# The down product of seven token pairs: another form of the seven-product scheme, with shared sums

## The chip, the core and the metric

The kernel runs on one core of a Trainium2 chip. The metric is the device time of one execution in microseconds; three runs of the kernel before gave 276.22, 276.23 and 276.27, median 276.23. The core has TensorE (PE in the profile, with its weight loads as PEld), VectorE (DVE), ScalarE (ACT), GpSimd (POOL) and SyncE (SP), which issues most of the transfers. Each engine works through its own list of instructions in order; waits between engines go over semaphores.

## The reference

Two layers on 2048 tokens of width 640, in bf16: a linear attention with 32 heads of width 20, and a gated product without a nonlinearity.

```python
qkv = layernorm(x) @ wqkv
phi_q = [softmax(q @ w_phi), softmax(-q @ w_phi)]        # per head; phi_k likewise
kv, z = sum over tokens of phi_k * v, of phi_k
o = (phi_q @ kv) / (phi_q @ z + 1e-6)
h = x + o @ wo
g, u = layernorm(h) @ w_gate, layernorm(h) @ w_up         # 640 -> 1536
out = h + (g * u) @ w_down                                # 1536 -> 640
```

The last line, the down product, is what is changed.

## The kernel before

Tokens are worked on in 16 tiles of 128, and the second layer in four blocks of four tiles (512 tokens). The work is cut into named units, and the names below are those of the lists in `ORDER`: `k`, `v` and `q` with a tile's number are its key, value and query products with their softmax, `K` and `Q` the sums and scalings of the feature maps, `A` the key-value product and `Aout` its copy, `n` the numerator and denominator of a tile, `h` its output product with the residual and the layer norm's statistics, `f0.3.2` the gate and up products of block 0, slice 3 of the hidden width (tokens from tile 2 of the block on), `T` the weight sums, `S` the block sums, `D1.0` the down product of the first pair of tiles in block 1, `d0` and `d1` the plain down product of tiles 0 and 1.

`ORDER` holds one list per engine, written out: the n-th occurrence of a unit's name on an engine is the n-th operation of that unit there. So it fixes the order on each engine in full. Nothing is moved at run time. Each operation carries a planned duration (`t`, `lat`) and `place` (L213) uses them to hand out buffers and to decide on which earlier operations each one waits; waits are made in `finish` (L302).

What the steps of the prediction touch:

- `fu` (L1068 on) makes one slice of the hidden layer: two products of five matmuls of 512 columns into one PSUM buffer of two banks, a copy of the gate half on ACT (L1077), the product of both on DVE (L1079). The buffer is free after DVE's step. There are four such buffers (`p_ps`), shared by all units.
- `queries` (L908 on): product, maximum and scaling on DVE (L872, L875), exponentials on ACT (L880), sums and reciprocal on DVE (L934, L940), two scalings on POOL (L941, L946).
- `num` (L992 on): products of 11 matmuls, then reciprocal (L1019) and scaling (L1021) on DVE.
- `watt` (L1027 on): output product of ten matmuls, two steps on DVE (L1050, L1053), square on ACT (L597), two steps on POOL (L1057, L1059, a power), the normalised rows `hb` on DVE (L1062), transposes issued by SP (L501).
- `weight_sums` (L1087): sums of quarters of `w_down` (768 x 320 each), one operation on POOL each (L1098), written into space that earlier weights and inputs leave.
- `block_sums` (L1101): sums of quarters of the hidden rows of a pair (each 128 tokens x 768), one operation on DVE each (L1110).
- `down_pair` (L1131): a pair's hidden rows (two tiles x two halves of the hidden width) times `w_down` (two halves x two halves of the columns) as a 2 x 2 block product by seven products instead of eight; a product is six matmuls of 320 columns (`mm`). Results that several blocks of the output need are copied from PSUM to `slot` by ACT (`snap`, L1161), combined on POOL (`padd`, L1167), and added to the remaining PSUM bank and written out by DVE (`fin`, L1172). A store of 160 KB per tile follows (L1177).

The pair of tiles 0 and 1 is done plainly (`down_raw`). In the form before, five block sums are made per pair, five weight sums in all, five copies per pair, and six additions on POOL per pair. Two of four last additions per pair wait for those on POOL.

Of the kernel before, what the change touches and what calls it, by code (L numbers as in the profile page):

```python
# [1318 lines left out]
```

## Time and profile before

| | |
|---|---|
| median of three runs | 276.23 us |
| profiled execution, first to last instruction | 274.27 us |
| TensorE busy | 266.2 us, 97% |
| VectorE busy | 202.0 us, 74% |
| ScalarE busy | 145.9 us, 53% |
| GpSimd busy | 147.9 us, 54% |
| granted TensorE clock | 1.000 |
| block sums (L1110) | 35, 23.7 us |
| copies (L1161) | 35, 15.3 us |
| weight sums (L1098) | 5, 19.3 us |

The profiled execution's own time is known by its span alone; the runs' times lie 1.96 us above it. A row of a group reads: line, engine, operation, written and read tiles, shapes, count, then busy time and the mean duration of one in ns, then the idle time ahead of it and what ended it. A row of the timeline reads: start and duration in us, engine, line, operation. The scratch tiles appear under the names of the memory that they lie in: the hidden rows as `phik`, block sums as `xT`, weight sums as `Wp` and `xT`, `w_down` as `vaug`, the copies as `eq` and `t`.

### The profile page before, as it was taken

What the parts mean: (1) busy time and instruction counts of PE and PEld (TensorE: products, weight loads), DVE (VectorE), ACT (ScalarE), POOL (GpSimd) and SP (SyncE); (2) the same over time, 40 slices, a digit from 0 to 9 for tenths busy, and PEclk for the clock granted to TensorE, in tenths of its full rate; (3) what the DMA queues carried; (4) which work ended last, traced back from release to release, by engine and by line L of the source; (5) the groups of instructions that cost most, each with busy time, mean ns of one, the idle gap of its engine ahead of it and who ended that gap; (6) DMA issues with size and microseconds to landing.
All of it is one profiled execution on the core that took longest, in us unless ns stands there. A gap on an engine that the chain in (4) does not pass through costs nothing.

```text
span 274.3 us, 5648 instructions
## 1 busy us (share of the span) xinstructions
PE 266.2 (97%) x2217; PEld 181.0 (66%) x2229; DVE 202.0 (74%) x388; ACT 145.9 (53%) x270; POOL 147.9 (54%) x187
## 2 busy tenths in 40 slices
PE   8999999999999999999999999999999999999992
PEld 8777776767868788788645557754554654456771
DVE  2899999999999989999855958555544565316772
ACT  3469999999676964776273422143342312332430
POOL 5437999999842365624899511621035330024895
PEclk9999999999999999999999999999999999999999
DMA  7988899803275897555564242620015101000112
GB/s 195 284 150 196 136 302 399 290 2 53 55 107 115 255 200 118 114 100 69 83 130 22 50 84 50 143 50 0 0 24 98 48 0 50 1 0 25 50 49 72
DMA packets 67099, 28.61 MB, mean 104 GB/s; under 512 B 57600, under 2 KB 65792, under 8 KB 67072
## 3 DMA queue, kind: packets, MB, share of 16 engines
q1 hardware_dynamic: 66144, 27.90, 44.9%
q10 hardware_dynamic: 928, 0.35, 0.5%
q8 instruction: 17, 0.28, 0.5%
q14 instruction: 10, 0.08, 0.1%
HBM read 11.82 MB, written 2.62 MB: 53 GB/s over the span
## 4 chain that ended last, share of the span: by engine, by line
PE 83%; POOL 6%; DVE 4%; DMA 2%; issue 2%; SPq 1%; ACT 1%; POOLq 0%; DVEq 0%
PE ps L604 83%; POOL eq L1167 4%; DMA Wp<-in_A_wqkv_dram 2%; POOL t L1167 2%; DVE ps L872 1%; DVE Sq L934 1%; SPq L501 1%; ACT phik L880 1%; DVE Ssum L894 0%; PE ps L512 0%; DVE Rk L896 0%; POOLq L371 0%; DVE x_all L1039 0%; DVE Phi L984 0%; SPq L497 0%
## 5 line engine op out<-in xcount | busy, mean ns | idle before, releaser
L604 PE MATMUL ps<-phik,Wgu 128*128 128x512 bf16 (+1 forms) x588 | 107.8, 335 | 0.6
L604 PEld LDWEIGHTS ps<-phik,Wgu 128*128 128x128 bf16 x600 | 58.1, 98 | 42.5 <-DVE phik L1079 1.2
L604 PE MATMUL ps<-Wp,xT 128*128 128x320 bf16 (+3 forms) x522 | 76.6, 299 | 0.2 <-ACT phik L880 0.2
L604 PEld LDWEIGHTS ps<-Wp,xT 128*128 128x128 bf16 x522 | 49.8, 98 | 19.5 <-ACT phik L880 0.7
L1079 DVE TENSOR_TENSOR phik<-ps,gate 128x512 bf16<-128x512 f32 (+1 forms) x60 | 34.0, 576 | 36.4 <-PE ps L604 29.9
L1077 ACT ACTIVATE gate<-ps 128x512 bf16<-128x512 f32 (+1 forms) x60 | 30.0, 511 | 53.8 <-PE ps L604 44.7
L897 POOL TENSOR_TENSOR phik<-phik,Rk 128x1280 bf16<-128x1280 bf16 x16 | 37.6, 2363 | 3.8 <-DVE Rk L896 3.0
L1167 POOL TENSOR_TENSOR eq<-eq 128x320 f32<-128x320 f32 x15 | 13.2, 881 | 33.1 <-ACT eq L1161 32.6
L872 DVE TENSOR_REDUCE ps<-ps 128x1 f32<-128x640 f32 (+1 forms) x32 | 26.1, 821 | 0.9 <-PE ps L604 0.3
L1161 ACT ACTIVATE eq<-ps 128x320 f32<-128x320 f32 x27 | 11.8, 438 | 27.0 <-PE ps L604 27.0
L1110 DVE TENSOR_TENSOR xT<-phik 128x768 bf16<-128x768 bf16 x35 | 23.7, 698 | 3.1 <-PE ps L604 3.1
L934 DVE TENSOR_REDUCE Sq<-eq 128x66 f32<-128x1320 bf16 x16 | 24.2, 1513 | 0.0
L894 DVE TENSOR_REDUCE Ssum<-phik 128x64 f32<-128x1280 bf16 x16 | 23.4, 1468 | 0.4 <-ACT phik L880 0.4
L1057 POOL TENSOR_SCALAR vpe<-shc 128x1 f32<-128x1 f32 x14 | 2.7, 192 | 36.4 <-ACT junk L597 36.1
L946 POOL TENSOR_TENSOR eq<-eq,rq 128x660 bf16<-128x660 bf16 x16 | 21.0, 1314 | 1.2
L597 ACT ACTIVATE junk<-x_all,nmh 128x640 bf16<-128x640 bf16 x14 | 11.6, 827 | 16.0 <-DVE x_all L1053 15.9
L880 ACT ACTIVATE eq<-ps,nb,rs 128x300 bf16<-128x300 f32 (+2 forms) x26 | 17.0, 687 | 5.4 <-DVE nb L875 4.6
L941 POOL TENSOR_TENSOR rq<-Sq,rq 128x33 f32<-128x33 f32 x16 | 4.5, 283 | 24.4 <-DVE rq L940 24.4
L604 PE MATMUL ps<-xT 128*128 128x320 bf16 (+1 forms) x144 | 17.4, 266 | 0.0
L880 ACT ACTIVATE eq<-ps,nb,nrs 128x300 bf16<-128x300 f32 (+2 forms) x26 | 17.2, 693 | 0.0
L880 ACT ACTIVATE phik<-ps,nb,rs 128x640 bf16<-128x640 f32 x16 | 14.2, 890 | 2.7 <-DVE nb L875 2.6
L604 PEld LDWEIGHTS ps<-xT 128*128 128x128 bf16 x144 | 11.8, 98 | 3.9 <-DVE xT L1110 0.2
(110 smaller groups left out, 374.9 us busy)
## 6 DMA issues: line engine op xcount, KB each, us to landing
x_all<-in_A_x_dram SPq DMA_DIRECT2D x4, 640.0 KB, 10.5
out_dram<-outb SPq DMA_DIRECT2D x16, 160.0 KB, 1.8
Wgu<-in_B_w_gate_dram SPq DMA_DIRECT2D x1, 1920.0 KB, 10.4
Wgu<-in_B_w_up_dram SPq DMA_DIRECT2D x1, 1920.0 KB, 15.8
vaug<-in_B_w_down_dram SPq DMA_DIRECT2D x1, 1920.0 KB, 9.0
Wp<-in_A_wqkv_dram SPq DMA_DIRECT2D x1, 800.0 KB, 4.9
phiqT<-in_A_wqkv_dram SPq DMA_DIRECT2D x1, 800.0 KB, 6.6
Wo<-in_A_wo_dram SPq DMA_DIRECT2D x1, 800.0 KB, 6.0
```

Of the source, the lines that this page charges most:

```text
L604: ins = e.matmul(o_, lhsT=l_, rhs=r_, start=s_, stop=p_, skip_group_check=True)
L872: g.op("DVE", lambda e: e.tensor_reduce(out=mx(), in_=src(), axis=AX.XY if len(src().shape) == 3 else AX.X, op=ALU.max, apply_absolute_val ...
L880: g.op("ACT", lambda e, s=s, sc=sc, to=to, of=of: e.activation(out=to(s), in_=of(), func=ACT.Exp, bias=nb[:, i:i + 1], scale=sc[:, t:t + 1 ...
L894: g.op("DVE", lambda e: e.tensor_reduce(out=Ssum[:, vs.i, :], in_=x, axis=AX.X, op=ALU.add), rd=R_phik[t], wr=vs.R, use=[vs], t=1.39, lat=1.5)
L897: g.op("POOL", lambda e: e.tensor_tensor(out=x, in0=x, in1=Rk[:, vr.i, :].unsqueeze(2).to_broadcast([P, 2 * H, DH]), op=ALU.mult), rd=vr.R ...
L934: g.op("DVE", lambda e: e.tensor_reduce(out=Sq[:, vs.i, :].rearrange("p (w g) -> p w g", w=NQ), in_=feat(0, NQ).rearrange("p w (g f) -> p ...
L946: return e.tensor_tensor(out=x, in0=x, in1=rq[:, vr.i, :].rearrange("p (w h) -> p w h", h=HW).unsqueeze(3).to_broadcast([P, NQ, HW, DH]), ...
L1077: g.op("ACT", lambda e: e.activation(out=gate[:, vg.i, 0:P * n], in_=PS[v.i][:, 0, 0:P * n], func=ACT.Copy), rd=[v.R[0]], wr=vg.R, use=[v, ...
L1079: g.op("DVE", lambda e: e.tensor_tensor(out=hhT[:, hb, ft, sl], in0=PS[v.i][:, 1, 0:P * n], in1=gate[:, vg.i, 0:P * n], op=ALU.mult), rd=[ ...
L1110: g.op("DVE", lambda e, k=k, x=x, y=y, op=op: e.tensor_tensor(out=SH[k][i], in0=part(x), in1=part(y), op=op), rd=rd, wr=[R_S[k][i]], t=0.6 ...
L1161: o = g.op("ACT", lambda e: e.activation(out=slot(x), in_=PS[v.i][:, bk, 0:HALF], func=ACT.Copy), rd=[v.R[bk]], wr=x.R, use=[v, x], after= ...
L1167: g.op("POOL", lambda e: e.tensor_tensor(out=slot(o_), in0=slot(a), in1=in1(), op=op), rd=a.R + r_, wr=o_.R, use=[o_, a] + ([y] if x is No ...
```

## The change

`down_pair` takes another form of the scheme, in which sums are built on each other: the third block sum uses the first, the fourth uses the third, and the weight sums likewise. There are four block sums per pair, four weight sums in all, seven products, and four copies per pair. The accumulation of products in one PSUM bank now makes most of the combinations: bank (v1, 0) takes products one, three and five one upon another and is copied after each. Each copy gets the residual added on POOL in place (one addition per copy, four per pair), and each of the four last additions on DVE reads one bank and one of those copies. The two stores of a pair change places. A copy may also be made by DVE, with the residual in the same step, where the table `SNAP` says so; it is empty, so all are made by ACT.

All five lists are new. On SP the loads keep their places; transposes and stores further on move with the units that they belong to. Three more edits: the weight and block sums take less of the old space (three weight slots and one in `xT`), the first exponential on ACT is counted as a user of the scratch tile it writes, and planned durations of the changed steps are set anew.

```diff
 def weight_sums():
-    for k, (a, b, op) in enumerate(((0, 3, ALU.add), (1, 3, ALU.subtract), (2, 0, ALU.subtract), (0, 1, ALU.add), (2, 3, ALU.add))):
+    for k, (a, b, op) in enumerate(((1, 0, ALU.subtract), (3, 1, ALU.subtract), (3, (0,), ALU.subtract), (2, (2,), ALU.subtract))):
...
 def block_sums(b, i):
-    for k, (x, y, op) in enumerate(((0, 3, ALU.add), (2, 3, ALU.add), (0, 1, ALU.add), (2, 0, ALU.subtract), (1, 3, ALU.subtract))):
+    for k, (x, y, op) in enumerate(((2, 3, ALU.add), (0, 2, ALU.subtract), ((0,), 0, ALU.subtract), (1, (2,), ALU.subtract))):
...
 def down_pair(b, i):
+    def snap(v, bk, t, half):
...
+        x.read = g.op("ACT", lambda e: e.activation(out=slot(x), in_=PS[v.i][:, bk, 0:HALF], func=ACT.Copy), rd=[v.R[bk]],
+                      use=[v, x], t=0.42, lat=0.55, **rw)
+        g.op("POOL", lambda e: e.tensor_tensor(out=slot(x), in0=slot(x), in1=x_all[:, t, c], op=ALU.add), rd=x.R + [R_h[t]],
+             wr=x.R, use=[x], t=0.87)
+        return x
+
+    def fin(v, bk, o_, half, y, after=None):
+        g.op("DVE", lambda e: e.tensor_tensor(out=outb[:, o_.i, HALF * half:HALF * (half + 1)], in0=PS[v.i][:, bk, 0:HALF], in1=slot(y),
+                                              op=ALU.add), rd=[v.R[bk]] + y.R, wr=[o_.R[half]], use=[v, o_, y],
+             after=[x.read for x in after or () if x.read], t=0.45, lat=0.57)
...
+    mm(v1, 0, raw(0), wraw(0), True, [v2])
+    a_ = snap(v1, 0, t1, 0)
+    mm(v2, 0, summed(0), wsum_(0), True)
+    d_ = snap(v2, 0, t2, 1)
+    mm(v1, 0, summed(2), wsum_(2), False)
+    b_ = snap(v1, 0, t1, 1)
+    mm(v1, 1, raw(1), wraw(2), True)
+    fin(v1, 1, o1_, 0, a_)
+    mm(v1, 0, summed(1), wsum_(1), False)
+    c_ = snap(v1, 0, t2, 0)
+    fin(v1, 0, o2_, 1, d_, [c_])
+    mm(v2, 1, raw(3), wsum_(3), True)
+    fin(v2, 1, o2_, 0, c_)
+    store(o2_, t2)
+    mm(v2, 0, summed(3), wraw(3), False)
+    fin(v2, 0, o1_, 1, b_)
+    store(o1_, t1)
```

The parts of the new lists that the prediction speaks of, from the place where block 1 begins to that of the first pair (`D0.1`):

```diff
 ORDER, "PE":
+ f1.10.0 f1.4.0 f1.10.0 f1.4.0 n14 f0.3.2 f0.3.2 h9 f1.3.0 f1.3.0 q13 f1.1.0 f1.1.0 f1.0.0 h14 f1.9.0 f1.0.0 f1.8.0 n11 f1.5.0
+ f1.9.0 f1.8.0 f1.7.0 f1.2.0 h10 f1.5.0 f1.2.0 n12 f1.7.0 d1 n13 f1.6.0 f1.6.0 h11 f1.11.0 f1.11.0 D0.1 D0.1 D0.1 n15 D0.1 D0.1 D0.1 D0.1
 ORDER, "DVE":
+ q15 f1.10.0 Q11 f0.0.2 Q15 n14 Q15 f0.3.2 S0.1.1 S0.1.0 h9 n14 f1.3.0 q13 h9 f1.4.0 q13 f1.1.0 h14 h14 S0.1.2 f1.0.0 n11 Q13 Q13 n11
+ f1.8.0 f1.9.0 S0.1.3 h9 h10 h10 f1.2.0 f1.7.0 n12 h8 f1.5.0 n13 d1 n12 n13 h10 h11 h11 f1.6.0 h11 n15 D0.1 f1.11.0
 ORDER, "ACT":
+ q15 q15 f1.10.0 q15 h8 f0.0.2 q15 d1 f0.3.2 f1.3.0 f1.4.0 f1.1.0 q13 h9 f1.0.0 q13 q13 q13 f1.8.0 f1.9.0 h10 f1.2.0 f1.5.0
 ORDER, "POOL":
+ Q12 Q12 Q11 h1 Q11 T0 h9 h9 T1 Q13 Q13 h8 Q15 Q15 h10 h10 h8 T2 T3 h11 h11 D0.1 D0.1 D0.1 h14 D0.1
```

In the lists before, POOL has `Q11 Q11 T2 T1 T0 h8 h8 T3 Q15` at this place and `T4` earlier, between `Q8` and `Q10`, and DVE has `S0.1.1 f0.5.0 S0.1.4` ahead of them and the next block sum, `S0.1.3`, after `f1.9.0`. At the end, the last two pairs are `D3.0` and `D3.1`; TensorE's new list ends with five products of the one and then the seven of the other; in the list before, the first two of `D3.1` stand among the last of `D3.0`.

More of the change, by code (lines that the diff above doesn't have):

```diff
@@ L58 @@
 ST_ACT = (12,)
+SNAP = {}
 SPLIT = [[(0, 2), (2, 2)], [(0, 4)], [(0, 4)], [(0, 4)]]
@@ L143, in __init__ @@
         self.R = [Reg() for _ in range(nreg)]
+        self.read = None
 class Op:
@@ L465, in _build @@
     Wkv = Wp[:, :, D:3 * D]
-    TW = [Wkv[:, 0:3, 0:2 * HALF], Wkv[:, 0:3, 2 * HALF:4 * HALF], Wkv[:, 3:5, 0:3 * HALF],
-          xTf[:, 0:KH * HALF].rearrange("p (a n) -> p a n", a=3), xTf[:, KH * HALF:2 * KH * HALF].rearrange("p (a n) -> p a n", a=3)]
-    o1 = 2 * KH * HALF
+    TW = [Wkv[:, 0:3, 0:2 * HALF], Wkv[:, 3:5, 0:3 * HALF], Wkv[:, 0:3, 2 * HALF:4 * HALF],
+          xTf[:, 0:KH * HALF].rearrange("p (a n) -> p a n", a=3)]
+    o1 = KH * HALF
     SH = [[xTf[:, o1 + KH * P * (2 * k + i):o1 + KH * P * (2 * k + i + 1)].rearrange("p (f n) -> p f n", f=KH) for i in range(2)]
-          for k in range(5)]
+          for k in range(4)]
     PS = [ctx.enter_context(nc.psum_tensor("ps%d" % i, [P, 2, 512], FP32)) for i in range(4)]
@@ L476, in _build @@
     p_hb, p_slot = Pool(2), Pool(8)
-    R_T, R_S = regs(5), [regs(2) for _ in range(5)]
+    R_T, R_S = regs(4), [regs(2) for _ in range(4)]
     SLOT_USERS = []
@@ L559, in _build @@
     pool_op(lambda e: e.memset(ones[:, :], SC / D), 0.2, wr=[R_one])
-    g.op("ACT", lambda e: e.activation(out=junk[:, 0, 0:1], in_=ones[:, 0:1], func=ACT.Exp), rd=[R_one], wr=[R_tab], t=1.4)
+    g.op("ACT", lambda e: e.activation(out=junk[:, 0, 0:1], in_=ones[:, 0:1], func=ACT.Exp), rd=[R_one], wr=[R_tab],
+         use=[Buf(p_junk)], t=1.4)
     pool_op(lambda e: e.memset(ident[:, :], 0.0), 0.2, wr=[R_id])
@@ L1087, in weight_sums, with part @@
         lo, hi = (0, HALF), (HALF, D)
-        for k, (a, b, op) in enumerate(((0, 3, ALU.add), (1, 3, ALU.subtract), (2, 0, ALU.subtract), (0, 1, ALU.add), (2, 3, ALU.add))):
-            U("T%d" % k)
-            def part(q, n):
-                f0, (c0, c1) = KH * (q // 2), (lo, hi)[q % 2]
-                return Wd[:, f0:f0 + KH, c0:c1].rearrange("p (a w) n -> p a w n", w=n)
-            def out_(n, k=k):
-                return TW[k].rearrange("p a (w n) -> p a w n", w=n)
+        def part(q, n):
+            if isinstance(q, tuple):
+                return TW[q[0]].rearrange("p a (w n) -> p a w n", w=n)
+            f0, (c0, c1) = KH * (q // 2), (lo, hi)[q % 2]
+            return Wd[:, f0:f0 + KH, c0:c1].rearrange("p (a w) n -> p a w n", w=n)
+        for k, (a, b, op) in enumerate(((1, 0, ALU.subtract), (3, 1, ALU.subtract), (3, (0,), ALU.subtract), (2, (2,), ALU.subtract))):
+            U("T%d" % k)
             n = TW[k].shape[2] // HALF
-            pool_op(lambda e, a=a, b=b, op=op, n=n, part=part, out_=out_: e.tensor_tensor(out=out_(n), in0=part(a, n), in1=part(b, n), op=op),
-                    4.0, rd=[R_Wd], wr=[R_T[k]])
+            rd = [R_Wd] + ([R_T[b[0]]] if isinstance(b, tuple) else [])
+            pool_op(lambda e, k=k, a=a, b=b, op=op, n=n: e.tensor_tensor(out=part((k,), n), in0=part(a, n), in1=part(b, n), op=op),
+                    4.0, rd=rd, wr=[R_T[k]])
     def block_sums(b, i):
@@ L1104, in part @@
         def part(q):
+            if isinstance(q, tuple):
+                return SH[q[0]][i]
             f0, c = KH * (q % 2), c0 + P * (q // 2)
             return hhT[:, hb_, f0:f0 + KH, c:c + P]
-        for k, (x, y, op) in enumerate(((0, 3, ALU.add), (2, 3, ALU.add), (0, 1, ALU.add), (2, 0, ALU.subtract), (1, 3, ALU.subtract))):
+        for k, (x, y, op) in enumerate(((2, 3, ALU.add), (0, 2, ALU.subtract), ((0,), 0, ALU.subtract), (1, (2,), ALU.subtract))):
             U("S%d.%d.%d" % (b, i, k))
-            rd = [R_hhT[hb_][ft][2 * i + q // 2] for q in (x, y) for ft in range(KH * (q % 2), KH * (q % 2) + KH)]
+            rd = [R_hhT[hb_][ft][2 * i + q // 2] for q in (x, y) if not isinstance(q, tuple)
+                  for ft in range(KH * (q % 2), KH * (q % 2) + KH)] + [R_S[q[0]][i] for q in (x, y) if isinstance(q, tuple)]
             g.op("DVE", lambda e, k=k, x=x, y=y, op=op: e.tensor_tensor(out=SH[k][i], in0=part(x), in1=part(y), op=op),
@@ L1157, in slot @@
             return eqf[:, HALF * x.i:HALF * (x.i + 1)] if x.i < 6 else t32[:, x.i - 6, :]
-        def snap(v, bk):
+        how = iter(SNAP.get((b, i), "AAAA"))
+        def snap(v, bk, t, half):
             x = Buf(p_slot)
-            o = g.op("ACT", lambda e: e.activation(out=slot(x), in_=PS[v.i][:, bk, 0:HALF], func=ACT.Copy), rd=[v.R[bk]], wr=x.R,
-                     use=[v, x], after=SLOT_USERS, t=0.42, lat=0.55)
-            return x, o
-        def padd(o_, a, y, op=ALU.add, x=None):
-            r_, in1 = (y.R, lambda: slot(y)) if x is None else ([R_h[x[0]]], lambda: x_all[:, x[0], HALF * x[1]:HALF * (x[1] + 1)])
-            g.op("POOL", lambda e: e.tensor_tensor(out=slot(o_), in0=slot(a), in1=in1(), op=op), rd=a.R + r_, wr=o_.R,
-                 use=[o_, a] + ([y] if x is None else []), t=0.72)
@@ L1170, in fin @@
-        def fin(v, bk, o_, t, y=None, after=()):
-            in1 = (lambda: slot(y)) if y is not None else (lambda: x_all[:, t, HALF * bk:HALF * (bk + 1)])
-            g.op("DVE", lambda e: e.tensor_tensor(out=outb[:, o_.i, HALF * bk:HALF * (bk + 1)], in0=PS[v.i][:, bk, 0:HALF], in1=in1(),
-                                                  op=ALU.add), rd=[v.R[bk], R_h[t]] + (y.R if y is not None else []), wr=[o_.R[bk]],
-                 use=[v, o_] + ([y] if y is not None else []), after=after, t=0.45, lat=0.57)
+            c = slice(HALF * half, HALF * (half + 1))
@@ new lines, in snap @@
+            rw = dict(wr=x.R, after=SLOT_USERS)
+            if next(how) == "V":
+                g.op("DVE", lambda e: e.tensor_tensor(out=slot(x), in0=PS[v.i][:, bk, 0:HALF], in1=x_all[:, t, c], op=ALU.add),
+                     rd=[v.R[bk], R_h[t]], use=[v, x], t=0.45, lat=0.57, **rw)
+                return x
+            x.read = g.op("ACT", lambda e: e.activation(out=slot(x), in_=PS[v.i][:, bk, 0:HALF], func=ACT.Copy), rd=[v.R[bk]],
+                          use=[v, x], t=0.42, lat=0.55, **rw)
@@ L1274, in _build @@
     each(queries, 3)
-    g.alias(R_T, R_Wp[1] + R_Wp[2] + R_xT[0:6])
+    g.alias(R_T, R_Wp[1] + R_Wp[2] + R_xT[0:3])
     weight_sums()
-    g.alias([r for x in R_S for r in x], R_xT[5:])
+    g.alias([r for x in R_S for r in x], R_xT[2:12])
     ffn(0)
```

24 lines of the change are left out of this document (1 added, 23 removed), and 96 rows, old and new, of the table ORDER.

## The prediction

> **What bounds the kernel now.** I read the page first, then the end of the timeline, then the timelines of VectorE (DVE) and GpSimd (POOL) beside each other, then the groups for durations.
>
> ```profile
> span 274.3 us, 5648 instructions
> PE 266.2 (97%) x2217; PEld 181.0 (66%) x2229; DVE 202.0 (74%) x388; ACT 145.9 (53%) x270; POOL 147.9 (54%) x187
> PE 83%; POOL 6%; DVE 4%; DMA 2%; issue 2%; SPq 1%; ACT 1%; POOLq 0%; DVEq 0%
> ```
>
> TensorE works 97% of the span and carries 83% of the chain, so whatever delays it adds to the time, and what other engines save is worth nothing by itself. The one stretch that it doesn't carry is the end, where the chain runs on POOL (6%). In timeline rows, the first number is the start, the second the duration:
>
> ```profile
> 265.60 0.98 PE L604 MATMUL ps<-Wp,phik 128*128 128x320 bf16 x6
> ...
> 266.41 0.98 PE L604 MATMUL ps<-vaug,xT 128*128 128x320 bf16 x6
> ...
> 267.23 1.80 PE L604 MATMUL ps<-xT 128*128 128x320 bf16 x12
> 267.43 0.44 ACT L1161 ACTIVATE eq<-ps 128x320 f32<-128x320 f32 x1 [0.37 <-PE ps L604]
> ...
> 269.59 1.80 POOL L1167 TENSOR_TENSOR eq<-eq 128x320 f32<-128x320 f32 x2
> 271.49 0.49 DVE L1172 TENSOR_TENSOR outb<-ps,eq 128x320 bf16<-128x320 f32 x1 [2.06 <-POOL eq L1167]
> ```
>
> The last product ends at 267.23 + 1.80 = 269.03. Then two additions on POOL, the last addition on DVE (to 271.98) and a store; the span ends at 274.27, 2.29 after DVE and 5.24 after TensorE. Two neighbouring products of six matmuls start 0.82 apart (265.60, 266.41), which is a product's real price; its row shows 0.16 more.
>
> **The change, part by part.** *Products.* Seven per pair before and after: 0. *Sums, copies, additions.* Per pair one block sum less on DVE, one copy less on ACT, two additions less on POOL, and over all one weight sum less on POOL.
>
> ```profile
> L1110 DVE TENSOR_TENSOR xT<-phik x35: 546/550/1675, 132.7 to 266.4; 128x768 bf16<-128x768 bf16 x35
> L1167 POOL TENSOR_TENSOR eq<-eq,x_all x9: 791/792/990, 171.3 to 268.7; 128x320 f32<-128x320 f32 x9
> L1098 POOL TENSOR_TENSOR xT<-vaug x2: 3815/3818/3822, 102.6 to 147.2; 128x1920 bf16<-128x1920 bf16 x2
> ```
>
> Seven pairs: 7 x 0.55 = 3.9 us of DVE, 7 x 0.44 = 3.1 us of ACT, 14 x 0.79 to 0.86 = 11 to 12 us of POOL, and 3.8 us of POOL for the weight sum. All of that lies under TensorE's work, except where POOL ends the chain: worth 0 before 269 us.
>
> *The end.* The new pair's third copy to be added (c_) is taken after product five of the last pair. With E the end of the last product, product five ends at E - 2 x 0.82 = E - 1.64; copy 0.44 and 0.03 of waiting: E - 1.17; POOL 0.07 + 0.79: E - 0.31; the addition to bank (v2, 1) is then in time for product six (E - 0.82) and runs E - 0.24 to E + 0.25; the last addition follows product seven at E + 0.25 or so and ends at E + 0.74. A store takes 2.29 from there to the span's end, and a first store half a microsecond ahead of it may cost 0.1: E + 3.1 instead of E + 5.24. **Term: -2.1 us.** POOL has no backlog there: the last two pairs have 8 additions x 0.79 = 6.3 us where 12 were needed. Bounds: -2.4 (the addition doesn't wait) to -1.6 (c_ waits one more addition).
>
> *Same-bank turnaround.* Products 1, 3 and 5 accumulate in one bank, with a copy between. In a run without other work the copy ends 0.98 + 0.03 + 0.44 = 1.45 after a product's start and the bank is wanted at 2 x 0.82 = 1.64. Slack 0.19: 0, with bounds 0 and +0.6 (six places where the new order leaves only one product between, 0.1 each).
>
> *The order.* Every engine's list is new (SP's loads keep theirs). The product count per block is the same, but one thing moves that the rows below price: where block sums, weight sums and normalisations meet.
>
> ```profile
> 132.68 0.55 DVE L1110 TENSOR_TENSOR xT<-phik 128x768 bf16<-128x768 bf16 x1
> ...
> 133.97 1.16 DVE L1110 TENSOR_TENSOR xT<-phik 128x768 bf16<-128x768 bf16 x1
> ```
> ```profile
> 133.41 1.31 POOL L946 TENSOR_TENSOR eq<-eq,rq 128x660 bf16<-128x660 bf16 x1
> 134.68 4.13 POOL L1098 TENSOR_TENSOR Wp<-vaug 128x1920 bf16<-128x1920 bf16 x1
> ```
> ```profile
> 157.02 1.68 DVE L1110 TENSOR_TENSOR xT<-phik 128x768 bf16<-128x768 bf16 x1
> ```
> ```profile
> 156.97 1.31 POOL L946 TENSOR_TENSOR eq<-eq,rq 128x660 bf16<-128x660 bf16 x1
> ```
> ```profile
> 204.66 0.78 DVE L1062 TENSOR_SCALAR hb<-x_all,nmh,rs 128x640 bf16<-128x640 bf16 x1 [2.72 <-DMA phik<-hb]
> ```
> ```profile
> 204.46 0.79 POOL L1167 TENSOR_TENSOR eq<-t,x_all 128x320 f32<-128x320 f32 x1
> ```
> ```profile
> 256.08 2.23 DVE L1110 TENSOR_TENSOR xT<-phik 128x768 bf16<-128x768 bf16 x2
> 256.91 0.99 POOL L1167 TENSOR_TENSOR eq<-eq,x_all 128x320 f32<-128x320 f32 x1
> ```
>
> A block sum takes 0.55. The one at 157.02 began 0.05 after a POOL operation of 1.31, took 1.68 and ended 0.41 after it (158.69 against 158.28): it stood still for the whole of it. The one at 133.97 ended 0.41 after POOL's 134.72, and the weight sum behind it took 4.13 instead of 3.82: whoever comes first holds the other up, and they take turns (256.08 and 256.91). The normalisation hb (L1062) does it too: it ended at 205.44, just after POOL's 205.25. The additions that read PSUM (L1172) don't show it. In the kernel before no block sum or normalisation starts inside one of the five weight sums; the cost that the lists carry for a block sum is a flat 0.6.
>
> The Trainium skill says the same ("SBUF — State Buffer", section "Who interferes with whom"): the only contention on the engines' side is a port pair of VectorE and GpSimd, held exclusively. The rows show it for holders of up to 1.31 us; for one of 3.82 us the rule has the whole of it and no row decides. By the rule T0's term below stands; if 1.31 us were the most that can be held, all three terms below would be 0 and the sum would be rival 1's.
>
> In the new lists DVE has "f1.10.0 Q11 f0.0.2 Q15 n14 Q15 f0.3.2 S0.1.1 S0.1.0 h9 n14 f1.3.0 q13" and POOL "Q11 h1 Q11 T0 h9 h9 T1". Durations:
>
> ```profile
> L1079 DVE TENSOR_TENSOR phik<-ps,gate 128x512 bf16<-128x512 f32 x36 | 24.4, 686 | 35.0 <-PE ps L604 28.7 <-ACT gate L1077 6.2
> L934 DVE TENSOR_REDUCE Sq<-eq 128x66 f32<-128x1320 bf16 x16 | 24.2, 1513 | 0.0
> ...
> L872 DVE TENSOR_REDUCE ps<-ps 128x1 f32<-128x640 f32 x26 | 21.1, 818 | 0.7 <-PE ps L604 0.3
> L1021 DVE TENSOR_TENSOR ob<-ps,rden 128x640 bf16<-128x640 f32 x14 | 11.4, 818 | 0.3
> L1053 DVE TENSOR_TENSOR x_all<-ps,x_all 128x640 bf16<-128x640 f32 x14 | 11.3, 814 | 0.0
> L1079 DVE TENSOR_TENSOR phik<-ps,gate 128x256 bf16<-128x256 f32 x24 | 9.6, 410 | 1.4 <-PE ps L604 1.1 <-ACT gate L1077 0.2
> ...
> L940 DVE RECIPROCAL rq<-Sq 128x33 f32<-128x33 f32 x16 | 5.5, 345 | 0.0
> ...
> L1019 DVE RECIPROCAL rden<-ps 128x32 f32<-128x32 f32 x14 | 5.0, 354 | 2.5 <-PE ps L604 2.5
> ```
> ```profile
> L946 POOL TENSOR_TENSOR eq<-eq,rq 128x660 bf16<-128x660 bf16 x16 | 21.0, 1314 | 1.2
> ...
> L1059 POOL TENSOR_TENSOR rs<-vpe,mhalf 128x1 f32<-128x1 f32 x14 | 7.8, 554 | 0.9
> ...
> L941 POOL TENSOR_TENSOR rq<-Sq,rq 128x33 f32<-128x33 f32 x16 | 4.5, 283 | 24.4 <-DVE rq L940 24.4
> ```
> ```profile
> 157.34 1.24 PE L604 MATMUL ps<-phik,Wgu 128*128 128x512 bf16 x5
> 158.42 1.53 PE L604 MATMUL ps<-Wo,phik 128*128 128x320 bf16 x10
> ...
> 164.11 0.50 PE L604 MATMUL ps<-Phi,phiqT 128*128 128x63 bf16 x11
> ```
>
> Count from r, the end of Q11's reciprocal. POOL: 0.1 + 0.28 + 0.55 + 1.31 and a little between: weight sum T0 starts at r + 2.35 and runs to r + 6.2. DVE (neighbours overlap by some 0.07): 0.34 + 1.44 + 0.28 + 0.28 + 0.34: S0.1.1 starts at r + 2.7 at the earliest, inside T0. Were it 0.4 earlier, T0 would have its turn after it and S0.1.0 would wait. Only 1 us earlier would both pass. So DVE stands about 3.4 us.
>
> What queues behind: the copies that free PSUM. All four PSUM buffers are then held, by f1.4.0, n14 and h9 (whose DVE steps stand behind the two sums) and by f1.3.0, and q13 needs one. DVE: T0's end r + 6.2, the two sums 0.41 + 0.47, h9's small step 0.1, n14's 0.75: n14's buffer is free at r + 7.95. TensorE, less 0.16 per row for the overlap: r is 0.05 + 0.69 + 0.28 = 1.0 after f1.10.0; then f1.4.0 1.08, n14 0.33, two of block 0 at half width 1.08, h9 1.37, f1.3.0 2.16: q13 is wanted at r + 5.0. **Term: +2.95**, say +3.0; bounds 0 (no meeting) and +3.4 (all of DVE's standstill).
>
> T1 meets S0.1.2 in the same way. After h9's addition on DVE, POOL's side needs about 0.8 (two DVE steps), then on ACT q13's first exponential and h9's square, and h9's two on POOL:
>
> ```profile
> L597 ACT ACTIVATE junk<-x_all,nmh 128x640 bf16<-128x640 bf16 x14 | 11.6, 827 | 16.0 <-DVE x_all L1053 15.9
> ...
> L597 ACT ACTIVATION_READ_ACCUMULATOR junk<-x_all,nmh 128x1 f32 x14 | 2.7, 190 | 0.0
> L880 ACT ACTIVATE eq<-ps,nb,rs 128x300 bf16<-128x300 f32 x10 | 6.0, 598 | 2.0 <-DVE nb L875 1.5 <-DMA phiqT<-eq 0.4
> ```
>
> 0.8 + 0.60 + 0.83 + 0.2 + 0.2 + 0.55 and 0.1 of waits = 3.3. S0.1.2 comes after h14: TensorE's f1.1.0, half of f1.0.0 and h14 (2.16 + 1.08 + 1.37 = 4.6 after q13), less the 1.75 in which DVE does q13's maximum and h9's addition (0.82 and 0.81 after 0.15), and 1.0 for h14's own two steps: 3.9. So T1 is 0.6 ahead and DVE stands 3.2 us; the buffer that goes missing is f1.0.0's. It comes free 0.41 + 0.65 after T1's end, 5.4 after h14's matmuls, and f1.5.0 wants it 3 x 1.08 + 0.33 = 3.6 after them: 1.8 reach TensorE. A margin of 0.6 in such a count isn't safe: bounds 0 and +1.8, **term +0.9**, the middle. T2 starts with the end of h8's power on POOL, for which h8's hb on DVE waits, so hb always finds T2 running; by the same count it asks 1.1 after T2's start and stands 2.7. Behind it is the step that frees f1.5.0's buffer, 0.85 later; f1.6.0 wants that buffer after d1 (24 matmuls, 3.3 us), which covers all but 1.1: bounds 0 and +1.1, **term +0.6**, the middle again. The first 80 us hold the same DVE work up to the key-value product, in nearly the same order: 0, bounds ±0.7.
>
> **Sum:** -2.1 + 3.0 + 0.9 + 0.6 = +2.4 on the profile's 274.27; the median shown, 276.23, has 1.96 around that span: 276.23 + 2.4 = **278.6 us**.
>
> **Rivals.** (1) *The end alone counts*: both sums pass before T0, or a long POOL operation lets VectorE in. For it: no row shows a sum inside a weight sum. Against: 157.02, and the count above. -2.1, and 0.2 for turnarounds: 274.3 us, faster. (2) *All three meet in full*: -2.1 + 3.0 + 1.8 + 1.1 = +3.8: 280.0 us. (3) *T0 alone, TensorE loses about 2*: it cancels the end, 276.2 us. For it: my count puts every wait on TensorE, and a buffer freed out of turn would soften it.
>
> **How the numbers follow.** Forecast 0.40 (with T0 and parts of the others, 277.0 to 279.4), rival 2 0.18, rival 3 0.08, rival 1 0.34. Slower by over 0.2% 0.58, within 0.2% (0.55 us, what a measurement here can tell from nothing) 0.08, faster 0.34. The cases have both signs, so the range is wide: 273.9 (rival 1 with the end at -2.4) to 280.4 (rival 2 and turnarounds); the forecast's own is 277.0 to 279.4.
>
> **What would show it.** Right: a block sum of over 3 us near 141 us that ends 0.4 after the first weight sum, and TensorE idle 2 to 3 us soon after, ahead of a query product; hb of over 1 us inside T2; 3.1 us from TensorE's end to the span's end. Wrong: block sums at 0.55 beside running weight sums, or both ahead of T0; TensorE without a wait between 130 and 180 us, which is rival 1; a tail of over 4 us, with POOL still adding.

## The result, and the profile after

The kernel after takes 282.40 us median (281.80 to 282.88) against 276.23 (276.06 to 276.42) beside it on the same chip: 2.2% slower, ratio 1.0221 [1.0207, 1.0234]. The forecast was 278.6, its range ended at 280.4. The profiled execution took 282.78, with a span of 280.7 (274.27 before): 6.4 us more. Line numbers grow by two to ten: L604 is now L606, L1098 L1101, L1110 L1116, L1062 L1064, L779 L781, L897 L899, L1167 L1177; in the experiments some are one more or less.

The page of the kernel after: span, busy times, TensorE in 40 slices of 7.0 us, its granted clock in the same slices, the chain.

```profile
span 280.7 us, 5607 instructions
PE 269.7 (96%) x2229; PEld 181.9 (65%) x2229; DVE 206.5 (74%) x381; ACT 141.5 (50%) x263; POOL 129.9 (46%) x172
...
PE   8999799999999999999988999999999999999995
...
PEclk9999999999999999999997999999999999999999
...
PE 73%; DVE 16%; issue 4%; DMA 2%; ACT 2%; SPq 1%; POOL 1%; POOLq 0%; DVEq 0%
```

DVE has 16% of the chain instead of 4%, POOL 1% instead of 6%. TensorE has two holes, one near 31 us and one near 147 us, and behind the second its clock falls. What it waited for (engine, line, releaser: total us, times, longest):

```profile
PE ps L606 <- DVE ob L1023: 2.6, 1, 2.6
PE ps L606 <- ACT Wp L810: 1.9, 1, 1.9
PE ps L606 <- DVE phik L1081: 1.4, 2, 0.8
```

The timeline of the kernel after at the first, second and third weight sum:

```profile
143.20 3.82 POOL L1101 TENSOR_TENSOR Wp<-vaug 128x1920 bf16<-128x1920 bf16 x1
143.63 4.27 DVE L1116 TENSOR_TENSOR xT<-phik 128x768 bf16<-128x768 bf16 x2
143.84 2.32 PE L606 MATMUL ps<-phik,Wgu 128*128 128x512 bf16 x10
148.75 2.18 PE L606 MATMUL ps<-Wp,xT 128*128 128x300 bf16 x10 [2.60 <-DVE ob L1023]
...
155.87 3.82 POOL L1101 TENSOR_TENSOR Wp<-vaug 128x1920 bf16<-128x1920 bf16 x1
157.43 2.67 DVE L1116 TENSOR_TENSOR xT<-xT,phik 128x768 bf16<-128x768 bf16 x1
160.75 4.49 PE L606 MATMUL ps<-phik,Wgu 128*128 128x512 bf16 x20 [0.60 <-DVE phik L1081]
...
170.97 3.81 POOL L1101 TENSOR_TENSOR Wp<-vaug,Wp 128x1920 bf16<-128x1920 bf16 x1
172.81 2.16 DVE L1064 TENSOR_SCALAR hb<-x_all,nmh,rs 128x640 bf16<-128x640 bf16 x1
175.63 1.68 PE L606 MATMUL ps<-phik,Wgu 128*128 128x512 bf16 x7 [0.77 <-DVE phik L1081]
```

T0 runs to 147.02. The two block sums issued 0.43 after its start end at 147.90 together; the groups of L1116 give the first as 3799 ns, so it ended at 147.43, 0.41 after T0:

```profile
L1116 DVE TENSOR_TENSOR xT<-phik x14: 545/552/3799, 143.6 to 267.2; 128x768 bf16<-128x768 bf16 x14
```

n14's scaling then frees the buffer for q13's product, which starts at 148.75. The bracket says 2.60; since neighbouring groups otherwise overlap by 0.16, the real loss is 2.76. In the same way T1 costs 0.60 + 0.16 = 0.76, and T2 0.77 + 0.16 = 0.93 (the expectations below count 0.73 and 0.90).

Directly behind q13's wait stands something the prediction didn't have. Windows of 10 us; behind the engines' busy times follows the granted clock, here 0.97 and 0.85:

```profile
140.00:150.00 10.00, 7.40 (x55) 4.45 (x54) 9.10 (x12) 3.37 (x8) 5.82 (x4) 0.97 0.13 25
150.00:160.00 10.00, 10.00 (x55) 4.91 (x53) 6.29 (x8) 4.21 (x9) 4.52 (x3) 0.85 0.27 54
```

10 x 0.03 + 10 x 0.15 = 1.8 us of clock are missing. The ten matmuls of q13 took 2.18, where the kernels without a long wait there have 1.53 for them. Not every execution had this: the mean granted clock of the five runs was 0.994, 0.994 and 0.993 in those of 282.78, 282.88 and 282.40, and 1.000 in those of 281.80 and 281.84. So the half clock is worth 0.6 to 1.1 us net, and the loss is 5.6 us without it.

The hole near 31 us also begins on VectorE. First the centring of the query weights as a group before and after (shortest, median, longest), then the timeline after:

```profile
L779 DVE TENSOR_SCALAR phiqT<-phiqT,nmeanq x3: 286/376/379, 19.7 to 26.2; 128x640 bf16<-128x640 bf16 x3
```
```profile
L781 DVE TENSOR_SCALAR phiqT<-phiqT,nmeanq x3: 378/1360/2360, 19.4 to 27.5; 128x640 bf16<-128x640 bf16 x3
...
27.36 4.75 POOL L899 TENSOR_TENSOR phik<-phik,Rk 128x1280 bf16<-128x1280 bf16 x2
27.54 2.36 DVE L781 TENSOR_SCALAR phiqT<-phiqT,nmeanq 128x640 bf16<-128x640 bf16 x1
...
32.13 0.88 ACT L882 ACTIVATE phik<-ps,nb,rs 128x640 bf16<-128x640 f32 x1 [2.11 <-DVE nb L877]
32.91 0.69 ACT L810 ACTIVATE Wp<-ps 128x640 bf16<-128x640 f32 x1
33.66 1.53 PE L606 MATMUL ps<-Wp,xT 128*128 128x320 bf16 x10 [1.85 <-ACT Wp L810]
```

A centring issued 0.18 after a key scaling on POOL (L899) stands until that has ended, VectorE's next maximum comes late, ScalarE's exponential waits 2.11 for it, and the copy L810 that frees TensorE's buffer stands behind that exponential. Before, the same centring (wq0) stood 0.16 ahead of the key scaling and took 0.38.

The end of the kernel after:

```profile
276.69 0.98 PE L606 MATMUL ps<-vaug,xT 128*128 128x320 bf16 x6
277.49 0.89 DVE L1182 TENSOR_TENSOR outb<-ps,eq 128x320 bf16<-128x320 f32 x2 [0.39 <-POOL eq L1177]
```

TensorE ends at 277.67, the span at 280.7: 3.0 instead of 5.24, -2.2.

### The profile page after: what moved, and what is told of

It is laid out like the page before. It is cut to its first block, busy times and chain, and to the rows that moved or that the text cites. A ratio compares the mean times of both kernels' runs of the same rounds, so it can differ in the third digit from the quotient of the medians.

```text
span 280.7 us, 5607 instructions
## 1 busy us (share of the span) xinstructions
PE 269.7 (96%) x2229; PEld 181.9 (65%) x2229; DVE 206.5 (74%) x381; ACT 141.5 (50%) x263; POOL 129.9 (46%) x172
## 4 chain that ended last, share of the span: by engine, by line
PE 73%; DVE 16%; issue 4%; DMA 2%; ACT 2%; SPq 1%; POOL 1%; POOLq 0%; DVEq 0%
PE ps L606 73%; DVE ps L874 2%; DVE Ssum L896 2%; DVE xT L1116 2%; DMA Wp<-in_A_wqkv_dram 2%; DVE phiqT L781 1%; DVE Wp L842 1%; DVE phik L1081 1%; DVE Sq L936 1%; SPq L502 1%; POOL eq L1177 1%; DVE Rk L898 1%; DVE hb L1064 1%; ACT junk L599 1%; DVE x_all L1055 1%
## 5 line engine op out<-in xcount | busy, mean ns | idle before, releaser
L606 PE MATMUL ps<-phik,Wgu 128*128 128x512 bf16 (+1 forms) x600 | 111.3, 339 | 1.4 <-DVE phik L1081 1.4
L606 PE MATMUL ps<-Wp,xT 128*128 128x320 bf16 (+1 forms) x606 | 89.6, 301 | 4.5 <-DVE ob L1023 2.6
L606 PEld LDWEIGHTS ps<-phik,Wgu 128*128 128x128 bf16 x600 | 58.2, 98 | 44.1 <-DVE phik L1081 2.2
L606 PEld LDWEIGHTS ps<-Wp,xT 128*128 128x128 bf16 x606 | 58.1, 98 | 28.8 <-DVE ob L1023 3.1
L899 POOL TENSOR_TENSOR phik<-phik,Rk 128x1280 bf16<-128x1280 bf16 x16 | 37.7, 2368 | 6.9 <-DVE Rk L898 6.3
L1177 POOL TENSOR_TENSOR eq<-eq,x_all 128x320 f32<-128x320 f32 x22 | 18.2, 836 | 38.4 <-ACT eq L1175 38.3
L606 PE MATMUL ps<-vaug,phik 128*128 128x63 bf16 (+1 forms) x308 | 26.2, 238 | 0.0
L606 PEld LDWEIGHTS ps<-vaug,phik 128*128 128x128 bf16 x308 | 18.5, 97 | 6.3 <-DVE phik L1081 0.2
L948 POOL TENSOR_TENSOR eq<-eq,rq 128x660 bf16<-128x660 bf16 x16 | 21.0, 1314 | 1.1
L1175 ACT ACTIVATE eq<-ps 128x320 f32<-128x320 f32 x22 | 9.3, 437 | 23.6 <-PE ps L606 23.6
L1182 DVE TENSOR_TENSOR outb<-ps,eq 128x320 bf16<-128x320 f32 x22 | 10.6, 487 | 10.3 <-PE ps L606 6.6
```

Of the source, the lines that this page charges most:

```text
L606: ins = e.matmul(o_, lhsT=l_, rhs=r_, start=s_, stop=p_, skip_group_check=True)
L899: g.op("POOL", lambda e: e.tensor_tensor(out=x, in0=x, in1=Rk[:, vr.i, :].unsqueeze(2).to_broadcast([P, 2 * H, DH]), op=ALU.mult), rd=vr.R ...
L948: return e.tensor_tensor(out=x, in0=x, in1=rq[:, vr.i, :].rearrange("p (w h) -> p w h", h=HW).unsqueeze(3).to_broadcast([P, NQ, HW, DH]), ...
L1177: g.op("POOL", lambda e: e.tensor_tensor(out=slot(x), in0=slot(x), in1=x_all[:, t, c], op=ALU.add), rd=x.R + [R_h[t]], wr=x.R, use=[x], t= ...
L1182: g.op("DVE", lambda e: e.tensor_tensor(out=outb[:, o_.i, HALF * half:HALF * (half + 1)], in0=PS[v.i][:, bk, 0:HALF], in1=slot(y), op=ALU. ...
```

## The experiments

My theory: the new lists let VectorE and GpSimd meet on their shared access to SBUF, at T0, T1 and T2 and in the first 40 us; all the loss is that and what follows from it. The rival: the new form or the new orders of the other engines cost TensorE time by themselves. Each kernel ran beside the kernel before (276.2 to 276.3).

**The front.** e1_front_before is the kernel after with the lists of before up to the first numerator.

```diff
-ORDER up to n0 / Aout / Q4: as after
+ORDER up to n0 / Aout / Q4: as before, all five engines
```

> The changed kernel with the lists of before up to the key-value product (PE and ACT up to the first n0, DVE up to Aout, POOL and SP up to the first Q4; the same operations stand there in both). Port theory (a VectorE operation with two SBUF inputs or in the fast copy form stands still while a POOL operation runs): the query weights' centring at 21.5 and 27.5 us goes back from 1.36 and 2.36 us to 0.3 to 0.4, TensorE's waits of 0.36 and 2.02 us at 29.5 and 31.5 go, 282.4 - 2.3 = 280.1 us; the stall of 2.76 us ahead of q13 stays. Rival (the front's order costs nothing, all is lost after 140 us): 282.4 us.

281.12, ratio 1.0170 [1.0148, 1.0191]; span 278.9, 1.8 less than after. The centrings are at their old duration and the 2 us hole is gone; q13's wait of 2.6 and, in three of the four runs, the half clock stay. The measured 281.1 lies between the two forecasts, so the front costs 1.3 to 1.8 here and the middle the rest.

**T0 and the first sums.** In e2_sums_after_T0 two block sums move on VectorE:

```diff
-f0.3.2 S0.1.1 S0.1.0 h9 n14 f1.3.0 q13 h9 f1.4.0 q13 f1.1.0
+f0.3.2 h9 n14 f1.3.0 q13 h9 f1.4.0 q13 S0.1.1 S0.1.0 f1.1.0
```

> The changed kernel with S0.1.1 and S0.1.0 moved on DVE alone, from behind f0.3.2 to behind q13's second step, where T0 has ended. Port theory: both take 0.55 us, TensorE's wait of 2.76 us ahead of q13 goes, and with it the half clock of 3.4 us behind it (1.7 us): 282.4 - 4.5 = 277.9 us, or up to 1 us more if T1 now meets S0.1.2 differently. Rival (DVE is simply late there, and the two sums cost what they take, 2 x 0.55): 282.4 - 1.1 = 281.3 us.

278.92, ratio 1.0097 [1.0078, 1.0117], 3.5 less than after, and 2.9 less than after's two runs at full clock, where the wait was 2.76. The wait ahead of q13 is gone and the clock stays full:

```profile
145.80 1.53 PE L606 MATMUL ps<-Wp,xT 128*128 128x300 bf16 x10
...
151.90 3.82 POOL L1101 TENSOR_TENSOR Wp<-vaug 128x1920 bf16<-128x1920 bf16 x1
152.78 3.35 DVE L1116 TENSOR_TENSOR xT<-xT,phik 128x768 bf16<-128x768 bf16 x1
156.79 3.41 PE L606 MATMUL ps<-phik,Wgu 128*128 128x512 bf16 x15 [1.29 <-DVE phik L1081]
```

Of the 1 us by which it missed 277.9, 0.69 is here: S0.1.2 now starts 0.88 after T1 instead of 1.56, stands longer, and T1 costs 1.29 + 0.16 = 1.45 instead of 0.76. The expectation had allowed for it.

In e3_half_T0 the other side is changed: half of T0's columns are left out, nothing is moved.

```diff
-out=part((k,), n), in0=part(a, n), in1=part(b, n)
+out=part((k,), n)[..., m], in0=part(a, n)[..., m], in1=part(b, n)[..., m]   # m: half of the columns for k = 0
```

> The changed kernel with half of the first weight sum T0 left out (half of its columns aren't computed), nothing moved. Port theory: T0 takes 1.9 us, S0.1.1 1.9 us in place of 3.8, TensorE's wait ahead of q13 shrinks by the same 1.9 to 0.85, too short for the half clock: 282.4 - 1.9 - 1.7 = 278.8 us. If the half clock comes with any such wait: 280.5. Rival (order and buffers, not the port): 282.4 us.

279.99, ratio 1.0133 [1.0116, 1.0151].

```profile
143.31 2.00 POOL L1102 TENSOR_TENSOR Wp<-vaug 128x960 bf16<-128x960 bf16 x1
143.74 2.45 DVE L1117 TENSOR_TENSOR xT<-phik 128x768 bf16<-128x768 bf16 x2
147.05 1.54 PE L606 MATMUL ps<-Wp,xT 128*128 128x300 bf16 x10 [0.78 <-DVE ob L1023]
```

T0 is 1.82 shorter, the pair of sums 1.82 shorter, TensorE's wait 1.82 shorter (2.60 to 0.78). So VectorE's standstill is T0's length and nothing else. The clock stays full. The time lies 1.2 above the expected 278.8. 0.7 of that is T1, which again costs 1.45; against after's runs at full clock (281.8) the time is 1.8 less, which is what T0 lost.

**All the meetings in the middle.** e5_no_meetings has the front of before, the weight sums in a row, and the four block sums taken from their places and put behind f1.9.0:

```diff
 POOL
-T0 h9 h9 T1 Q13 Q13 h8 Q15 Q15 h10 h10 h8 T2 T3
+T0 T1 T2 T3 h9 h9 Q13 Q13 h8 Q15 Q15 h10 h10 h8
 DVE
-f1.9.0 S0.1.3 h9 h10 h10 f1.2.0
+f1.9.0 S0.1.1 S0.1.0 S0.1.2 S0.1.3 h9 h10 h10 f1.2.0
```

> The changed kernel with the front lists of before, with T1, T2 and T3 right behind T0 on POOL and with the four block sums of pair 0.1 behind f1.9.0 on DVE, past all four. Port theory: no wait of TensorE over 0.6 us after 85 us, clock 1.000, the shorter end stays: 282.4 - 2.3 - 2.76 - 1.7 - 0.73 - 0.90 = 274.0 us, faster than before (276.2). Rival (order and buffers): not under 277 us.

276.21, ratio 0.9992 [0.9966, 1.0019]: no difference from before, between the two forecasts.

```profile
157.94 1.67 DVE L1116 TENSOR_TENSOR xT<-phik 128x768 bf16<-128x768 bf16 x2
...
160.23 1.55 DVE L1116 TENSOR_TENSOR xT<-phik,xT 128x768 bf16<-128x768 bf16 x1
...
162.99 0.51 PE L606 MATMUL ps<-Phi,phiqT 128*128 128x63 bf16 x11 [0.60 <-DVE x_all L1055]
```

The sums are out of the weight sums and in the two 1.3 us scalings of Q13 and Q15 (L948, 157.4 to 161.4). VectorE is late for h10's buffer, and two new waits of 0.77 (0.60 + 0.16, rounded) and 0.81 appear. e6_sums_spread differs in one list:

```diff
-f1.9.0 S0.1.1 S0.1.0 S0.1.2 S0.1.3 h9 h10 h10 f1.2.0 ... h11 h11 f1.6.0
+f1.9.0 h9 h10 h10 S0.1.1 S0.1.0 f1.2.0 ... h11 h11 S0.1.2 S0.1.3 f1.6.0
```

> The new form with the first stretch's lists of before and the four weight sums in a row as in e5_no_meetings, but the four block sums of pair 0.1 are spread on VectorE: two behind h10's second step, two behind h11's second step, away from Q13 and Q15 on GpSimd. If e5 lost its gain only to the two waits of 0.77 and 0.81 us behind block sums that stood still for 1.2 and 1.5 us, these go: 276.2 - 1.6 = 274.6 us (274.2 to 275.2). Rival, that the new form costs TensorE time of its own wherever its sums stand: 276 or more.

275.15 (274.42 to 276.24), ratio 0.9954 [0.9934, 0.9973]: both waits gone, and the new form faster than before, at the upper end of what was expected.

**The front by itself, two ways.** e7_two_centrings is the kernel after with two operations moved on VectorE:

```diff
-wq4 K0 K3 wq2 k2 K3 k2 s4 s4 s4 s4 s4 K1 k7 K1 k7 wq0 k4
+wq4 wq2 K0 K3 k2 K3 k2 s4 s4 s4 s4 s4 wq0 K1 k7 K1 k7 k4
```

> The kernel after with two centrings of the query weights moved on VectorE alone: wq2 directly behind wq4, wq0 ahead of the first step of K1. All else in the new lists stays. If the front's loss is VectorE standing while GpSimd scales keys (2.36 us each), the centrings take 0.3 to 0.4 us again instead of 1.36 and 2.36, TensorE's waits of 0.36 and 2.02 us near 30 us go or shrink to under 0.5 together, and the time is 280.2 to 281.1 us. Rival, that the front's loss comes from the new order of TensorE or ScalarE: 282.2 to 282.6, with the 2.02 us wait kept.

280.32, ratio 1.0142 [1.0108, 1.0176], as the theory had it; the wait near 31 us is gone.

```profile
L781 DVE TENSOR_SCALAR phiqT<-phiqT,nmeanq 128x640 bf16<-128x640 bf16 x3 | 1.1, 381 | 0.2 <-DMA phiqT<-in_A_wqkv_dram 0.2
```

Two operations on one engine give back at least what all five lists of before did in e1: 2.1 by the medians and 1.3 by the spans, against 1.3 and 1.8. In e12_new_front_alone only the front's meetings are left: the middle of e6 behind the untouched front of after.

```diff
-e6_sums_spread, ORDER up to n0 / Aout / Q4: as before
+e6_sums_spread, ORDER up to n0 / Aout / Q4: as after
```

> e6_sums_spread with the first stretch's lists of the kernel after, so that all that is left of the loss is the front's: the centrings stand still for 1.36 and 2.36 us and TensorE waits 0.36 and 2.02 us. If the losses add up, 275.15 + 1.3 to 1.9 = 276.4 to 277.1 us, and the clock stays full after the 2.02 us wait. Rival, that a late start is made good later (TensorE catches up on waits): 275.0 to 275.6.

276.67, ratio 1.0016 [1.0007, 1.0026]; span 274.8 against e6's 272.7. The front costs 1.5 by the medians, 2.1 by the spans; it isn't made good later. Its wait of 1.85 left the clock at full.

**The new lists with nine operations moved.** e10_five_moves_kept_front joins the moves of e7, e5 (POOL) and e6 in the kernel after; everything else keeps the new lists.

```diff
 DVE: wq2 and wq0 as in e7, S0.1.1 S0.1.0 S0.1.2 S0.1.3 as in e6
 POOL
-T0 h9 h9 T1 ... T2 T3
+T0 T1 T2 T3 h9 h9 ...
```

> The kernel after with its own new lists everywhere, in which only these are moved: two centrings (as in e7_two_centrings), three weight sums right behind the first (as in e5_no_meetings), and four block sums (as in e6_sums_spread). If meetings on the port are all that the new lists cost, it comes to e6's time: 274.4 to 275.8 us, faster than before. Rival, that the new lists of TensorE and ScalarE in the first 130 us cost time of their own: 276.2 or more.

274.43 (274.15 to 275.40), ratio 0.9942 [0.9923, 0.9960]: 8.0 us faster than after and 1.8 faster than before. Between e10 and e12 only the two centrings differ: 274.43 against 276.67, spans 272.3 against 274.8. So the front's two meetings cost 2.2 to 2.5 us, with everything else alike.

```profile
span 272.3 us, 5607 instructions
PE 267.4 (98%) x2229; PEld 181.7 (67%) x2229; DVE 196.0 (72%) x381; ACT 141.3 (52%) x263; POOL 130.0 (48%) x172
...
268.27 0.98 PE L606 MATMUL ps<-vaug,xT 128*128 128x320 bf16 x6
```

TensorE ends at 269.25, where it ended before (269.03), and the span 3.05 later: what is left of the change is its end. The rival, that the form or TensorE's new order costs something, is out: the same products in the same order, with copies between accumulations, cost 0.2 net.

**The kernel before, made slow.** e9_before_planted moves one block sum of the kernel before into its run of three weight sums:

```diff
-f0.5.0 S0.1.4 q15 q13 f1.3.0 q15 q13 f1.10.0 f1.8.0 Q15
+f0.5.0 q15 q13 f1.3.0 q15 q13 f1.10.0 f1.8.0 S0.1.4 Q15
```

> The kernel BEFORE with one block sum moved on VectorE: S0.1.4 from behind f0.5.0 to behind f1.8.0, into the stretch in which GpSimd runs three weight sums one behind another (134.7 to 146.4 us). There VectorE is idle for 1.5 us, so a block sum of 0.55 us would cost nothing: 276.2 us if the rival holds. If a block sum stands still for a whole weight sum, it takes 3.5 to 4.3 us, the next gate product on VectorE (due 140.1) comes up to 2.7 us late, and TensorE waits 0.5 to 2.5 us: 276.7 to 278.7 us.

276.19, ratio 0.9993 [0.9981, 1.0006]: no difference, the rival's number, but not for the rival's reason.

```profile
134.81 11.69 POOL L1097 TENSOR_TENSOR Wp<-vaug 128x1920 bf16<-128x1920 bf16 x3
140.85 1.97 DVE L1109 TENSOR_TENSOR xT<-phik 128x768 bf16<-128x768 bf16 x1
144.56 0.68 DVE L1078 TENSOR_TENSOR phik<-ps,gate 128x512 bf16<-128x512 f32 x1
```

The same gate product in the kernel before:

```profile
144.43 0.69 DVE L1079 TENSOR_TENSOR phik<-ps,gate 128x512 bf16<-128x512 f32 x1 [1.79 <-PE ps L604]
```

The sum did stand still (1.97 instead of 0.55), for the rest of the second weight sum. But VectorE had 1.79 idle ahead of its next gate product, which hides a standstill of 1.4. The place was badly chosen to see a price. e13_before_two_planted moves the second sum there too:

```diff
-n9 S0.1.1 f0.5.0 q15 q13 f1.3.0 q15 q13 f1.10.0 f1.8.0 S0.1.4 Q15
+n9 f0.5.0 q15 q13 f1.3.0 q15 q13 f1.10.0 f1.8.0 S0.1.1 S0.1.4 Q15
```

> The kernel BEFORE with both block sums S0.1.1 and S0.1.4 moved on VectorE to behind f1.8.0, where one of them alone stood still for 1.4 us and cost nothing because VectorE had 1.8 us idle behind it. The second has to let the rest of a further weight sum pass: it ends near 146.7 us instead of 142.8, VectorE is about 4 us late, and TensorE's next buffers come 1.5 to 3 us late: 277.5 to 279.3 us. Rival, that both sums pass in the gap between two weight sums or under VectorE's idle time: 276.2 to 276.6 us.

281.46, ratio 1.0190 [1.0175, 1.0206].

```profile
141.03 5.68 DVE L1109 TENSOR_TENSOR xT<-phik 128x768 bf16<-128x768 bf16 x2
149.15 2.04 PE L603 MATMUL ps<-phik,Wgu 128*128 128x512 bf16 x5 [3.37 <-DVE phik L1078]
...
140.00:150.00 10.00, 6.63 (x30) 2.81 (x29) 9.23 (x7) 4.24 (x9) 9.85 (x5) 0.97 0.26 52
150.00:160.00 10.00, 10.00 (x64) 5.15 (x63) 5.72 (x9) 2.27 (x5) 3.42 (x5) 0.86 0.27 18
```

The old form, with one operation more in the wrong place, is as slow as the new one: a wait of 3.37 + 0.16 = 3.5 and 10 x 0.03 + 10 x 0.14 = 1.7 of lost clock make 5.2, and 281.46 - 276.26 is 5.2. I expected 277.5 to 279.3; the mechanism was right, the wait was underrated, and the clock was left out of the sum a second time, although after's trace had shown it.

**When the clock falls.** e8_seven_eighths_T0 and e11_fifteen_sixteenths_T0 are the edit of e3 with 7/8 and 15/16 of T0's columns kept.

> The kernel after with an eighth of the columns of the first weight sum T0 left out (its output is then not the reference's): T0 about 3.35 us instead of 3.82, S0.1.1 about 3.35 instead of 3.80, and the wait ahead of q13 about 2.3 instead of 2.76. If any wait of over 2 us halves the clock for some 3.4 us, the half clock comes again: 281.9 us (281.6 to 282.2). If it takes more than 2.3 us of a wait, or hangs on where the wait lies: clock at full, 280.2 us (279.9 to 280.7).

> The kernel after with a sixteenth of the columns of T0 left out (output not the reference's): the wait ahead of q13 about 2.55 us, between the 2.30 that left the clock at full and the 2.76 that halved it for 3.4 us. If the length of the wait decides, either is possible, and it narrows the bound; half clock: 282.2 (281.9 to 282.7); full clock: 281.2 us (280.6 to 281.6), its first later wait then growing from 0.73 to 1.2 to 1.4.

281.63, ratio 1.0193 [1.0156, 1.0230], and 281.92, ratio 1.0212 [1.0193, 1.0231]. First e8's row, then e11's with the window behind it:

```profile
148.17 1.54 PE L606 MATMUL ps<-Wp,xT 128*128 128x300 bf16 x10 [2.13 <-DVE ob L1023]
```
```profile
148.84 1.54 PE L606 MATMUL ps<-Wp,xT 128*128 128x300 bf16 x10 [2.37 <-DVE ob L1023]
...
150.00:160.00 10.00, 8.71 (x55) 4.54 (x54) 7.83 (x11) 4.84 (x10) 4.53 (x3) 1.00 0.28 55
```

Neither profile shows the half clock; the four with waits of 2.60 (after, e1, e7) and 3.37 (e13) do. But the mean granted clock is known for every run, the unprofiled ones too. A half rate of 3.4 us takes 1.7 off a span of 280, so it makes the mean 0.994. In the new form the runs read either 0.993 to 0.994 or 0.998 to 1.000, and nothing between:

| kernels | wait ahead of q13 in the profile | runs at 0.993 to 0.994 |
|---|---|---|
| after, e1, e7 | 2.59 to 2.60 | 8 of 13 (3 of 5, 3 of 4, 2 of 4) |
| e11 | 2.37 | 1 of 4 (282.68) |
| e8 | 2.13 | 1 of 4 (283.15) |
| e3 | 0.78 | 0 of 4 |
| e2, e5, e6, e10, e12 | none | 0 of 37 |

In the old form the mean can't be read so: e9's profile has a half rate behind the last matmul, where it costs nothing. So the same kernel has the half clock in some executions and not in others, and one profile of each sets no threshold. Without it e8 took 281.22 to 281.76 and e11 281.57 to 281.96. Taking e8's and e11's shorter waits (0.47 and 0.23) off after's 281.82 at full clock gives 281.35 and 281.59. The forecasts for full clock, 280.2 and 281.2, were too low since T1's wait grows to 1.45 in both: TensorE now arrives earlier at the buffer that S0.1.2 keeps. For e8 I had left that out, though e3 had shown it. The times alone don't tell the two cases apart: of e7's two runs with the half clock one is its slowest (281.53) and one its fastest (279.84).

The half rate doesn't begin at the same place either. First after, then e7, in windows of 1 us, and q13 in e7:

```profile
149.00:150.00 1.00, 1.00 (x8) 0.63 (x6) 0.29 (x1) 0.00 (x0) 0.00 (x0) 0.75 0.06 13
```
```profile
146.00:147.00 1.00, 0.00 (x0) 0.00 (x0) 1.00 (x4) 0.00 (x0) 0.00 (x0) 0.82 0.00 0
...
147.13 2.85 PE L606 MATMUL ps<-Wp,xT 128*128 128x300 bf16 x10 [2.59 <-DVE ob L1023]
```

In after it begins at 149.5, 0.75 behind q13's start; in e7 at 146.6, 0.5 ahead of it, while TensorE still waits. In all four profiles it lasts 3.4 us. In after and e1 the next wait, T1's, shrinks by 0.7 (0.60 and 0.59 in the brackets, against 1.29 at full clock), so the half clock's 1.8 is 1.1 net; in e7 T1's bracket is 1.19, so that saving isn't general.

## Why the prediction was wrong

The direction was right and the middle's three terms were near; what failed is the term of the first 80 us, set to 0. Step by step:

- *End, -2.1*: measured -2.2. Right, and alone in e10: -1.8 by the medians, where rival 1 had 274.3 and e10 gives 274.43. That sum was right for lists without a meeting. (The spans of those runs differ by 2.1: runs of the new form lie 2.0 to 2.1 above their spans, runs of the old 1.7 to 1.8. The prediction took 1.96 for both, so 0.3 us was missing there, and where it goes isn't shown.)
- *T0, +3.0 (2.95)*: measured 2.76. The block sum of over 3 us, ending 0.4 after T0, and the idle TensorE ahead of a query product were there; the first stood at 143.6, not near 141, since the front's loss had moved it (in e1 it stands at 141.8). e3 shows cause and proportion: 1.82 off T0 is 1.82 off the wait. The longest holder the rows of before had was 1.31; the Trainium skill's rule ("SBUF — State Buffer", section "Who interferes with whom") that the pair is held for the whole instruction agrees with the trace up to 3.8 us.
- *T1, +0.9*, and *T2, +0.6*: measured 0.76 and 0.93, inside their bounds, sum 1.7 against 1.5. T1's isn't a constant: 1.45 in e2, e3, e8 and e11, where TensorE or VectorE came earlier. Meetings don't simply add.
- *Same-bank turnaround, 0*: right; e10's TensorE ends within 0.2 of before.
- ***First 80 us, 0, bounds ±0.7***: this step failed. It said that the same DVE work stands there "in nearly the same order". The order that matters isn't VectorE's own but VectorE's against POOL's. Two centrings were let in behind key scalings of 2.36 us, and it cost 1.3 (e1, medians) to 2.5 (e12 against e10, spans), two to three times the bound of 0.7. The text priced block sums and hb as the victims and never asked which other steps of VectorE go from SBUF to SBUF; the centring (bf16 in, bf16 out, no PSUM) was one. The same section of the Trainium skill names such a `tensor_scalar` among those that can take the shared pair; the trace agrees, 378 against 2360 ns.
- ***T0's term a second time***: mis-sized by what follows the wait. The sum treated 3.0 us of an idle TensorE as 3.0 us. The half clock behind it took 1.8 more in the profiled execution, some 0.7 of which T1's smaller wait gave back. It came in three of five runs, and the two without it, at 281.8, lie outside the range as well.

Sum by the profile: -2.2 + 2.76 + 0.76 + 0.93 + 1.8 (clock) = 4.05, and 2.1 to 2.5 for the front (e12 against e6 and against e10, spans): 6.2 to 6.6, and the span grew by 6.4. Without the clock and the front it is 2.25, the forecast's +2.4. The range ended at 280.4, which is rival 2 and 0.4 for turnarounds. It left out the prediction's own upper bounds of the end, of T0 and of the first 80 us; with all of them the sum is -1.6 + 0.6 + 3.4 + 1.8 + 1.1 + 0.7 = +6.0, or 282.2. The front's own bound, worked out from a row (two centrings x up to 2.36 of standstill), would have reached past that.
